# Attention features in a fused performer and mixture kernel: the shift's arithmetic rewritten, one scaling, three copies and one group of sums put elsewhere

## The chip, the core and the metric

The kernel runs on one core of a Trainium2 chip. A core has five engines that run their own instruction queues side by side and wait for each other by semaphores: TensorE (PE, matmuls; its weight loads are shown as PEld), VectorE (DVE), ScalarE (ACT), GpSimd (POOL) and SyncE (SP, which here only issues DMAs). The metric is the device time of one execution in microseconds (us). Before the change it is 640.66 us, the median of three runs (640.45 to 641.06).

## What is computed

Three layers follow each other. The first is linear attention with random features over 2 batches, 8 heads, 576 tokens of 64 numbers, with 128 features:

```python
def phi(x):
    proj = np.einsum('bhsd,md->bhsm', x, omega)
    sq = np.sum(x * x, axis=-1, keepdims=True) / 2.0
    h = proj - sq
    h = h - np.max(h, axis=-1, keepdims=True)
    return np.exp(h) / np.sqrt(m)
q_p, k_p = phi(q_s), phi(k_s)          # q_s, k_s: q and k scaled
kv = einsum('bhsm,bhsd->bhmd', k_p, v); z = sum(k_p, axis=2)
num = einsum('bhsm,bhmd->bhsd', q_p, kv)
den = einsum('bhsm,bhm->bhs', q_p, z)[..., None] + 1e-06
out = num / den
```

The second is a mixture of four experts on the 1152 tokens of width 512 (each: 512 to 1024, relu, 1024 to 512, weighted and summed). The third takes 512 to 2048, multiplies each value by its cosine, and goes back to 512.

## The kernel before, in words

The order of the instructions on each engine is the order in which the Python code is run; generators are advanced by hand, and each `yield` marks a place where other work is put in between. There is no scheduler behind it.

The attention works on eight pairs of heads (`pairs`, line 1139), four tokens per partition, and a ninth part for the tokens that are left over (qL, kL). The loop over `s` from line 1356 is a pipeline: in step `s` it finishes the sums of keys and values of pair `s-1` (`kv_of`, line 1155), turns the queries of pair `s` and the keys of pair `s+1` (`turn_ahead`, line 1279, output `xT`), makes the features of both (`features`, line 1058), and writes the result of pair `s-2`. From `s = 6` on (`first`, line 1259) quanta of the expert layer's matmuls (`dense_quanta`) are put between the attention's.

The features of one pair need a shift per token. GpSimd squares the 64 numbers of each token and adds them in halves down to 16 (`norms_ahead`, lines 1017 and 1021), then multiplies these 16 by a constant (line 1024). VectorE adds the 16 (line 1074), takes the maxima of the projections from PSUM (line 1080), and then forms the shift from a tile `three` of three numbers for each token with two reductions over two neighbouring numbers each (lines 1089 and 1092); the second writes `nb`. ScalarE's exponentials (line 1099, output `phk` or `phq`) take `nb` as their bias. There are 17 such shifts: nine for queries (q0 to q7 and qL) and eight for keys (k0 to k7). The kL part makes its shift otherwise. For the keys of steps before `first`, `shift_later` puts a yield between the maxima and the two reductions, so that on VectorE the next step's copy of `xT` comes in between.

In the expert layers each quantum is six matmuls. `token_sums` (line 338) makes sums of blocks of the tokens (tiles T1, T2 and so on, each as a high and a low part), and one of its two calls, for the columns that begin at 1, is advanced a quantum at a time once attention is over (lines 1444 and 1445). `Second.ahead` stages the inputs of the second matmuls (`sth` on ScalarE at line 749, `stl` on VectorE at line 752).

Of the kernel before, what the change touches and what calls it, by code (L numbers as in the profile page):

```python
# [12 lines left out]
ACTF = mybir.ActivationFunctionType  # L13
ALU = mybir.AluOpType
AX = mybir.AxisListType
# [11 lines left out]
def performer_moe_kernel(ctx, tc, q, k, v, omega, probs, w1, w2, w_in, w_out, out):  # L27
    nc = tc.nc
# [16 lines left out]
    SC = float(D) ** -0.25  # L45
# [16 lines left out]
    def bank(name):  # L62
        return ps.tile([P, 512], F32, tag="ps", name=name)
# [218 lines left out]
    def tokens(n, ks, cols):  # L282
        return [t[:, ks, HALF * n + cols.start : HALF * n + cols.stop, :] for t in x_t]
# [4 lines left out]
    def whole(r, parts):  # L288
        h, l = (x.bitcast(F32) for x in parts)
        nc.vector.tensor_tensor(out=r, in0=h, in1=l, op=ALU.add)  # L290

    def minus(dst, x, y):
        nc.vector.tensor_tensor(out=dst, in0=x, in1=y, op=ALU.subtract)  # L293
# [5 lines left out]
    def less(r, n, ks, cols):  # L299
        h, l = (x.bitcast(F32) for x in tokens(n, ks, cols))  # L300
        minus(r, h, r)
        nc.vector.tensor_tensor(out=r, in0=r, in1=l, op=ALU.add)
# [35 lines left out]
    def token_sums(cols):  # L338

        r1, r2 = spare(cols)  # L340
        whole(r2, tokens(0, LO, cols))
        whole(r1, tokens(1, LO, cols))
        if not cols.start:
            yield
        minus(r1, r1, r2)
        yield
        parts = sum_out(1, r1, cols)
        next(parts)
        yield
        yield from parts  # L350
        less(r1, 1, HI, cols)
        yield
        yield from rest_sums(r1, r2, cols)
# [596 lines left out]
    with tc.tile_pool(name="at1", bufs=1) as at1, tc.tile_pool(name="at2", bufs=2) as at2:  # L950
# [63 lines left out]
        def norms_ahead(nm, t):  # L1014

            x2 = at2.tile([P, 2 * R, D], F32, tag=f"x2{nm[0]}", name=f"x2_{nm}")
            nc.gpsimd.tensor_tensor(out=x2, in0=t, in1=t, op=ALU.mult)
            w = D
            while w > 16:
                w //= 2  # L1020
                nc.gpsimd.tensor_tensor(
                    out=x2[:, :, 0:w], in0=x2[:, :, 0:w], in1=x2[:, :, w : 2 * w], op=ALU.add
                )
            nc.gpsimd.tensor_scalar(
                out=x2[:, :, 0:w], in0=x2[:, :, 0:w], scalar1=-SC * SC / 2, scalar2=None, op0=ALU.mult
            )
            sqs[nm] = x2[:, :, 0:w]

        def turn(nm, t, pieces=1):
# [28 lines left out]
        def features(nm, turned, phi, squares=None, shift_later=False):  # L1058

            nb = at2.tile([P, 2 * R], F32, tag=f"nb{nm}"[:3], name=f"nb_{nm}")  # L1060
            pjs = [bank(f"pj_{nm}_{g}") for g in range(2)]
            for i in range(R):
                c = slice(i * P, (i + 1) * P)
                for z, (x_, y) in enumerate([(turned, ws)] + [(squares, minus_norm)] * (squares is not None)):
                    for g, pj in enumerate(pjs):
                        r = slice(g * D, (g + 1) * D)
                        nc.tensor.matmul(
                            pj[:, i * M : (i + 1) * M], x_[r, c], y[r, :],
                            start=z == 0, stop=z == (squares is not None),
                        )  # L1070
            yield
            three = at2.tile([P, 2 * R, 3], F32, tag=f"th{nm[0]}", name=f"three_{nm}")
            def square_sum():
                nc.vector.tensor_reduce(out=three[:, :, 1], in_=sqs.pop(nm), op=ALU.add, axis=AX.X)

            if squares is None and nm != "q0":
                square_sum()
            for g, pj in enumerate(pjs):
                to = (nb if squares is not None else three[:, :, 0])[:, g : 2 * R : 2]
                nc.vector.tensor_reduce(  # L1080
                    out=to, in_=pj.rearrange("p (a m) -> p a m", m=M), op=ALU.max, axis=AX.X,
                    negate=squares is not None,
                )
            if shift_later:
                yield
            if squares is None:
                if nm == "q0":
                    square_sum()
                nc.vector.tensor_reduce(
                    out=three[:, :, 2], in_=three[:, :, 0:2], op=ALU.add, axis=AX.X, negate=True  # L1090
                )
                nc.vector.tensor_reduce(out=nb, in_=three[:, :, 1:3], op=ALU.add, axis=AX.X)
            yield
            order = [g + 2 * i for g in range(2) for i in range(R)]
            if squares is not None:
                order.insert(1, order.pop(R))
            for ix in order:
                i, g = divmod(ix, 2)
                nc.scalar.activation(  # L1099
                    phi[:, ix, :], pjs[g][:, i * M : (i + 1) * M], ACTF.Exp, bias=nb[:, ix : ix + 1]  # L1100
                )
# [38 lines left out]
        NPR = len(pairs)  # L1140
        xss, phks, phqs, kts, qts = {}, {}, {}, {}, {}

        kv = [at1.tile([P, 2, B, D + 1], F32, name=f"kv{hp}") for hp in range(NP)]
# [11 lines left out]
        def kv_of(i):  # L1155
            b, hp = pairs[i]
            ve, phk = ves[i % 2], phks.pop(i)
            kvp = room.pop() if room else bank(f"kv_{i}")
            kvp = kvp[:, 4 * (D + 1) : 6 * (D + 1)].rearrange("p (h e) -> p h e", h=2)
            for h in range(2):  # L1160
                for r in range(R):
                    column_halves(kvp[:, h, :], phk[:, h * R + r, :], ve[:, h * R + r, :], h == r == 0, False)
            yield
            for h in range(2):
                n = 2 * hp + h
                column_halves(kvp[:, h, :], phiL[:, n, :], veL[:, n, b, :], False, h == 1)
            yield
            nc.vector.tensor_copy(out=kv[hp][:, :, b, :], in_=kvp)

        pTs = {}  # L1170
        room = []
# [77 lines left out]
        for b in range(B):  # L1249
            nc.sync.dma_start(  # L1250
                out=pr[:, b * R : (b + 1) * R, :],
                in_=probs[b * S : b * S + SB, :].rearrange("(p r) e -> p r e", r=R),
            )
            nc.sync.dma_start(
                out=pr[b * L : (b + 1) * L, NTILE - 1, :], in_=probs[b * S + SB : (b + 1) * S, :]
# [3 lines left out]
        first = 6  # L1259
# [47 lines left out]
        def k_features(s, shift_later=False):  # L1307
            phks[s] = at2.tile([P, 2 * R, M], F32, tag="phk", name=f"phk_{s}")
            return features(f"k{s}", turned.pop(("k", s)), phks[s], shift_later=shift_later)
# [45 lines left out]
        ks, ns = iter(()), iter(())  # L1355
        for s in range(NPR + 3):
# [4 lines left out]
            else:  # L1361
# [28 lines left out]
                if 2 <= s <= NPR + 1:  # L1390
                    b, hp = pairs[s - 2]
                    px = put_x(f"{s - 2}", hp, xss.pop(s - 2), b * R, R)
                qs = q_features(s) if s <= NPR else iter(())
                ks = k_features(s + 1, s < first) if s + 1 < NPR else iter(())
                next(qs, None)
                next(ks, None)
                next(px, None)
# [34 lines left out]
            if s == first:  # L1432
                nc.vector.reciprocal(out=psum_, in_=psum_)
                nc.vector.tensor_tensor(
                    out=pn, in0=pr, in1=psum_.to_broadcast([P, NTILE, E]), op=ALU.mult
# [40 lines left out]
```

## Time and profile before

| what | value |
|---|---|
| median of three runs | 640.66 us |
| the profiled execution | 640.92 us |
| its span, first to last instruction | 639.1 us |
| TensorE's granted clock, mean | 0.999 of full speed |
| busy share of the span: PE, DVE, ACT, POOL | 99%, 76%, 55%, 27% |
| first matmul of the expert layers (g at line 549) | starts at 52.3 us |

Shares over the whole span say little here, since the change touches only the first 100 us. A table of the engines' busy time by stretches of 10 us is therefore read first, then the chain of waits within the first 100 us, then the order of time around single instructions. A busy PE counts modelled ends of matmuls, so idle time in PE is also seen in the spacing of their starts.

### The profile page before, as it was taken

The page shows a single profiled execution, that of the slowest core. Times are in us where ns is not written, and L with a number is a line of the kernel's source. Part 1 is how long each engine was busy: PE and PEld are TensorE (multiplying, and loading weights), DVE is VectorE, ACT ScalarE, POOL GpSimd, SP SyncE. Part 2 cuts the span into 40 slices and gives each one's busy share as a digit, 9 for nine tenths or more (in the row PEclk, how much of TensorE's full clock was granted, in tenths as well). Part 3 has the DMA queues.
Part 4 walks back from the last instruction along what each step waited for, and adds up shares of the span by engine and source line. Part 5 has one row for each costly group of instructions (what it writes and reads, how often), then busy time and mean ns, then how long its engine had stood idle before and what let it go on. Part 6 is the DMA issues. An engine that isn't in the chain of part 4 may idle for free.

```text
span 639.1 us, 10296 instructions
## 1 busy us (share of the span) xinstructions
PE 632.7 (99%) x3871; PEld 536.3 (84%) x3871; DVE 488.7 (76%) x877; ACT 353.3 (55%) x686; POOL 174.4 (27%) x217
## 2 busy tenths in 40 slices
PE   9999999999999999999999999999999999999997
PEld 8889988988888888888888888888888888888887
DVE  6998588789688688598687697699698772687842
ACT  6898664365346454354443455544457973476821
POOL 7899752033332333323333232310000000000000
PEclk9999999999999999999999999999999999999999
DMA  7644431313446433446334435301250002500111
GB/s 184 169 123 144 134 99 32 101 67 132 132 148 206 141 113 135 133 141 220 133 99 132 143 125 211 131 34 67 94 202 34 2 0 96 234 2 2 49 50 49
DMA packets 55442, 70.97 MB, mean 111 GB/s; under 512 B 15201, under 2 KB 40033, under 8 KB 55393
## 3 DMA queue, kind: packets, MB, share of 16 engines
q1 hardware_dynamic: 46800, 40.92, 20.3%
q0 software_dynamic: 8448, 29.37, 13.2%
q8 instruction: 30, 0.49, 0.3%
q14 instruction: 20, 0.16, 0.1%
q10 hardware_dynamic: 144, 0.03, 0.0%
HBM read 55.36 MB, written 14.94 MB: 110 GB/s over the span
## 4 chain that ended last, share of the span: by engine, by line
PE 86%; ACT 4%; DVE 4%; POOL 3%; issue 1%; DMA 1%; DVEq 0%; ACTq 0%; POOLq 0%
PE g L779 44%; PE g_odd L585 4%; PE g_1c L549 2%; PE g_0a L549 2%; PE g_3a L549 2%; PE g_2a L549 2%; PE g_1a L549 2%; PE g_2c L549 2%; PE g_3c L549 2%; PE g_0c L549 2%; ACT phk L1099 1%; PE g_0d L549 1%; PE g_0b L549 1%; PE g_3e L549 1%; PE g_3b L549 1%
## 5 line engine op out<-in xcount | busy, mean ns | idle before, releaser
L749 ACT ACTIVATE sth<-h 128x512 fp32r<-128x512 f32 (+1 forms) x111 | 60.3, 554 | 80.1 <-PE g L779 67.2
L258 POOL TENSOR_TENSOR c<-c 128x512 uint32<-128x512 uint32 x32 | 47.2, 1475 | 86.8 <-issue 34.0
L752 DVE SCALAR_TENSOR_TENSOR stl<-h,sth 128x512 fp32r<-128x512 f32 (+1 forms) x72 | 49.1, 697 | 26.7 <-ACT sth L749 26.6
L779 PE MATMUL g<-v2h,stl 128*128 128x512 f32 (+1 forms) x110 | 42.5, 386 | 0.6 <-DVE stl L752 0.6
L779 PE MATMUL g<-v3h,sth 128*128 128x512 f32 (+1 forms) x110 | 42.9, 390 | 0.0
L779 PE MATMUL g<-v0h,sth 128*128 128x512 f32 (+1 forms) x110 | 42.7, 388 | 0.0
L779 PE MATMUL g<-v1h,sth 128*128 128x512 f32 (+1 forms) x110 | 42.7, 388 | 0.0
L779 PE MATMUL g<-v2h,sth 128*128 128x512 f32 (+1 forms) x110 | 42.5, 386 | 0.0
L779 PE MATMUL g<-v0h,stl 128*128 128x512 f32 (+1 forms) x110 | 42.5, 386 | 0.0
L779 PE MATMUL g<-v3h,stl 128*128 128x512 f32 (+1 forms) x110 | 42.4, 386 | 0.0
L779 PE MATMUL g<-v1h,stl 128*128 128x512 f32 (+1 forms) x110 | 42.4, 386 | 0.0
L779 PE MATMUL g<-v1l,sth 128*128 128x512 f32 (+1 forms) x110 | 42.4, 385 | 0.0
L779 PE MATMUL g<-v0l,sth 128*128 128x512 f32 (+1 forms) x110 | 42.4, 385 | 0.0
L779 PE MATMUL g<-v3l,sth 128*128 128x512 f32 (+1 forms) x110 | 42.4, 385 | 0.0
L779 PE MATMUL g<-v2l,sth 128*128 128x512 f32 (+1 forms) x110 | 42.4, 385 | 0.0
L293 DVE TENSOR_TENSOR stl<-h,sth 128x512 fp32r<-128x512 f32 (+1 forms) x39 | 22.8, 593 | 19.3 <-ACT sth L749 19.1
L451 DVE SCALAR_TENSOR_TENSOR c<-c 128x512 f32<-128x512 f32 (+1 forms) x38 | 25.0, 662 | 11.9 <-ACT c L449 11.8
L448 ACT ACTIVATE c<-h 128x512 f32<-128x512 f32 x32 | 19.9, 622 | 19.9 <-DVE h L626 19.9
L805 DVE SCALAR_TENSOR_TENSOR acc<-g,pn,acc 128x512 f32<-128x512 f32 x27 | 20.1, 744 | 6.5 <-PE g L779 6.5
L779 PEld LDWEIGHTS g<-v2h,stl 128*128 128x128 f32 x110 | 20.7, 188 | 5.1 <-DVE stl L752 1.0
L779 PEld LDWEIGHTS g<-v0h,stl 128*128 128x128 f32 x110 | 20.7, 188 | 4.4 <-DVE stl L752 0.3
L779 PEld LDWEIGHTS g<-v3h,stl 128*128 128x128 f32 x110 | 20.7, 188 | 4.2
(437 smaller groups left out, 1877.3 us busy)
## 6 DMA issues: line engine op xcount, KB each, us to landing
rv<-in_moe_w_dram SPq DMA_DIRECT2D x16, 512.0 KB, 4.0
c<-in_moe_w_in_dram POOLq DMA_DIRECT2D x16, 512.0 KB, 4.1
c<-in_moe_w_out_dram POOLq DMA_DIRECT2D x16, 512.0 KB, 3.9
kt<-in_k_dram SPq DMA_DIRECT2D x8, 256.0 KB, 3.7
qt<-in_q_dram SPq DMA_DIRECT2D x8, 256.0 KB, 4.0
ve<-in_v_dram SPq DMA_DIRECT2D x16, 128.0 KB, 4.2
ra_2as<-in_moe_w_dram SPq DMA_DIRECT2D x8, 256.0 KB, 3.3
out_dram<-acc SPq DMA_DIRECT2D x7, 256.0 KB, 2.3
```

Source lines behind the costliest of these rows:

```text
L258: nc.gpsimd.tensor_tensor(out=total, in0=t, in1=lw, op=ALU.add)
L293: nc.vector.tensor_tensor(out=dst, in0=x, in1=y, op=ALU.subtract)
L448: nc.scalar.activation(vv, src, ACTF.Copy, bias=0.25, scale=INV_2PI)
L451: nc.vector.scalar_tensor_tensor(out=vv, in0=kk, scalar=ROUND, in1=vv, op0=ALU.subtract, op1=ALU.subtract)
L549: nc.tensor.matmul(dst, x[:, o], y[:, kk], start=start and n == 0, stop=stop and n == 3 * kn - 1, skip_group_check=reopen,)
L585: nc.tensor.matmul(g, x[:, kk], w[:, :, :, kk, :], start=n == 0, stop=n == 3 * KD - 1)
L749: nc.scalar.activation(hi, src, ACTF.Relu if self.e < E else ACTF.Copy)
L752: nc.vector.scalar_tensor_tensor(out=to, in0=src, scalar=0.0, in1=hi.bitcast(F32), op0=ALU.max, op1=ALU.subtract)
L779: nc.tensor.matmul(g, x, y[:, o : o + w], start=n == 0, stop=n == 3 * FT - 1)
L805: nc.vector.scalar_tensor_tensor(out=acc[t], in0=src, scalar=p_, in1=acc[t], op0=ALU.mult, op1=ALU.add)
L1099: nc.scalar.activation(phi[:, ix, :], pjs[g][:, i * M : (i + 1) * M], ACTF.Exp, bias=nb[:, ix : ix + 1])
```

## The change

Four things are changed.

1. GpSimd's multiplication by the constant (line 1024) is gone, 17 instructions. The constant is put into VectorE's two instructions of the shift, which become two `scalar_tensor_tensor` in place of two `tensor_reduce`. Both take two inputs from the tile `three`, which lies in SBUF.
2. The copy of the sums of keys and values out of PSUM (line 1168) is made by ScalarE for pairs 1, 2 and 3 (in steps 2, 3 and 4), by VectorE for the others as before.
3. `shift_later` isn't passed any more: the keys' shift stands right behind their maxima in all steps.
4. In `token_sums`, for the columns that begin at 1, there is one more yield ahead of `less(r1, 1, HI, cols)`.

```diff
@@ token_sums
         next(parts)
         yield
         yield from parts
+        if cols.start:
+            yield
         less(r1, 1, HI, cols)
@@ norms_ahead
-            nc.gpsimd.tensor_scalar(
-                out=x2[:, :, 0:w], in0=x2[:, :, 0:w], scalar1=-SC * SC / 2, scalar2=None, op0=ALU.mult
-            )
             sqs[nm] = x2[:, :, 0:w]
@@ features
-                nc.vector.tensor_reduce(
-                    out=three[:, :, 2], in_=three[:, :, 0:2], op=ALU.add, axis=AX.X, negate=True
-                )
-                nc.vector.tensor_reduce(out=nb, in_=three[:, :, 1:3], op=ALU.add, axis=AX.X)
+                for out, x, op in ((three[:, :, 2], three[:, :, 0], ALU.add), (nb, three[:, :, 2], ALU.subtract)):
+                    nc.vector.scalar_tensor_tensor(
+                        out=out, in0=three[:, :, 1], scalar=-SC * SC / 2, in1=x, op0=ALU.mult, op1=op
+                    )
@@ kv_of
-            nc.vector.tensor_copy(out=kv[hp][:, :, b, :], in_=kvp)
+            if i in (1, 2, 3):
+                nc.scalar.activation(kv[hp][:, :, b, :], kvp, ACTF.Copy)
+            else:
+                nc.vector.tensor_copy(out=kv[hp][:, :, b, :], in_=kvp)
@@ the loop over s
-                ks = k_features(s + 1, s < first) if s + 1 < NPR else iter(())
+                ks = k_features(s + 1) if s + 1 < NPR else iter(())
```

On VectorE, at the turn from step 1 to step 2, the order before is this (the numbers behind the names are buffers; `pj_k` are the projections, `tp` the turned inputs, `rd` and `xs` the division, `tq` the turned features):

```order
L1080 TENSOR_REDUCE three_k_441<-pj_k_1_426 128x4
L1303 COPY xT_522<-tp_0_504 128x8x64
L1089 TENSOR_REDUCE three_k_441<-three_k_441 128x8
L1092 TENSOR_REDUCE nb_k_424<-three_k_441 128x8
L1110 TENSOR_SCALAR rd_0_557<-num_1_464 128x4
L1110 TENSOR_SCALAR rd_1_559<-num_0_473 128x4
L1112 RECIPROCAL rd_0_557<-rd_0_557 128x4
L1112 RECIPROCAL rd_1_559<-rd_1_559 128x4
L1114 TENSOR_TENSOR xs_463<-num_1_464,rd_0_557 128x4x64
L1114 TENSOR_TENSOR xs_463<-num_0_473,rd_1_559 128x4x64
L1168 COPY kv_141<-num_1_464 128x2x65
L1182 COPY pT_0_566<-tq_0_539 128x512
```

The same place of VectorE's queue after the change:

```order
L1079 TENSOR_REDUCE three_k_436<-pj_k_1_421 128x4
L1089 SCALAR_TENSOR_TENSOR three_k_436<-three_k_436 128x8
L1089 SCALAR_TENSOR_TENSOR nb_k_419<-three_k_436 128x8
L1305 COPY xT_517<-tp_0_499 128x8x64
L1109 TENSOR_SCALAR rd_0_550<-num_1_459 128x4
L1109 TENSOR_SCALAR rd_1_552<-num_0_468 128x4
L1111 RECIPROCAL rd_0_550<-rd_0_550 128x4
L1111 RECIPROCAL rd_1_552<-rd_1_552 128x4
L1113 TENSOR_TENSOR xs_458<-num_1_459,rd_0_550 128x4x64
L1113 TENSOR_TENSOR xs_458<-num_0_468,rd_1_552 128x4x64
L1184 COPY pT_0_559<-tq_0_532 128x512
```

The shift stands ahead of the copy of `xT`, its two instructions are of another kind, and the copy of `kv` has left this queue.

On GpSimd, for the queries of pair 3 and the keys of pair 4, before:

```order
L1017 TENSOR_TENSOR x_q_621<-qt_3_484 128x512
L1021 TENSOR_TENSOR x_q_621<-x_q_621 128x8x32
L1021 TENSOR_TENSOR x_q_621<-x_q_621 128x8x16
L1024 TENSOR_SCALAR x_q_621<-x_q_621 128x8x16
L1017 TENSOR_TENSOR x_k_626<-kt_0_482 128x512
L1021 TENSOR_TENSOR x_k_626<-x_k_626 128x8x32
L1021 TENSOR_TENSOR x_k_626<-x_k_626 128x8x16
L1024 TENSOR_SCALAR x_k_626<-x_k_626 128x8x16
```

And after:

```order
L1019 TENSOR_TENSOR x_q_616<-qt_3_479 128x512
L1023 TENSOR_TENSOR x_q_616<-x_q_616 128x8x32
L1023 TENSOR_TENSOR x_q_616<-x_q_616 128x8x16
L1019 TENSOR_TENSOR x_k_620<-kt_0_477 128x512
L1023 TENSOR_TENSOR x_k_620<-x_k_620 128x8x32
L1023 TENSOR_TENSOR x_k_620<-x_k_620 128x8x16
```

Each set of squares is three instructions in place of four.

On VectorE at the end of attention, where `h` names a free buffer that `token_sums` uses for its sums and `c` and `acc` hold inputs of the second matmuls, before:

```order
L293 TENSOR_TENSOR h<-h 128x2x384
L752 SCALAR_TENSOR_TENSOR stl<-c_97,sth 128x512
L134 TENSOR_TENSOR T1l<-h,T1h 128x2x384
L293 TENSOR_TENSOR h<-xh,h 128x2x384
L302 TENSOR_TENSOR h<-h,xl 128x2x384
L752 SCALAR_TENSOR_TENSOR stl<-c_97,sth 128x256
L752 SCALAR_TENSOR_TENSOR stl<-acc_100,sth 128x256
L293 TENSOR_TENSOR h<-h 128x2x384
L134 TENSOR_TENSOR T2l<-h,T2h 128x2x384
```

And after:

```order
L293 TENSOR_TENSOR h<-h 128x2x384
L754 SCALAR_TENSOR_TENSOR stl<-c_97,sth 128x512
L134 TENSOR_TENSOR T1l<-h,T1h 128x2x384
L754 SCALAR_TENSOR_TENSOR stl<-c_97,sth 128x256
L754 SCALAR_TENSOR_TENSOR stl<-acc_100,sth 128x256
L293 TENSOR_TENSOR h<-xh,h 128x2x384
L302 TENSOR_TENSOR h<-h,xl 128x2x384
L293 TENSOR_TENSOR h<-h 128x2x384
L134 TENSOR_TENSOR T2l<-h,T2h 128x2x384
```

The two `stl` now stand ahead of the two sums of `less`. On ScalarE the evacuation `acc` (line 803) likewise moves ahead of `T2h`. The queues of PE and SP are the same in both kernels.

## Rows read from the trace of the kernel before

**Rows 1.** The page's first two lines: the span, and each engine's busy us (share).

```profile
span 639.1 us, 10296 instructions
PE 632.7 (99%) x3871; PEld 536.3 (84%) x3871; DVE 488.7 (76%) x877; ACT 353.3 (55%) x686; POOL 174.4 (27%) x217
```

**Rows 2.** Stretches of 10 us: length, busy us of each engine (instructions), PE clock, DMA.

```profile
20.00:30.00 10.00, 9.73 (x212) 8.57 (x208) 9.31 (x34) 8.87 (x31) 8.95 (x14) 1.00 0.62 166
...
40.00:50.00 10.00, 9.90 (x223) 9.01 (x220) 9.66 (x34) 9.55 (x32) 9.18 (x13) 1.00 0.27 78
...
70.00:80.00 10.00, 10.00 (x106) 9.24 (x107) 5.52 (x20) 5.55 (x16) 7.08 (x7) 1.00 0.52 157
```

**Rows 3.** The chain of waits, first 120 us: start us, us, engine, tile, line.

```profile
21.13 0.68 DVE xT L1303
...
28.11 0.60 DVE xT L1303
...
30.06 0.20 DVE kv L1168
...
36.19 2.24 ACT phk L1099 x8
...
48.70 0.66 DVE xT L1303
```

**Rows 4.** Groups of POOL's instructions, first 72 us: xcount | busy us, mean ns.

```profile
L1017 POOL TENSOR_TENSOR x_q<-qt 128x512 f32<-128x512 f32 x8 | 8.3, 1040 | 0.5
...
L1021 POOL TENSOR_TENSOR x_q<-x_q 128x256 f32<-128x256 f32 x9 | 6.6, 731 | 0.7
...
L1024 POOL TENSOR_SCALAR x_q<-x_q 128x128 f32<-128x128 f32 x9 | 4.8, 529 | 0.8
L1024 POOL TENSOR_SCALAR x_k<-x_k 128x128 f32<-128x128 f32 x8 | 4.2, 530 | 0.7
L1021 POOL TENSOR_TENSOR x_q<-x_q 128x128 f32<-128x128 f32 x9 | 4.1, 459 | 0.7
```

**Rows 5.** The order of time near 32 us: start us, us, engine, line, instruction.

```profile
30.93 0.53 POOL L1024 TENSOR_SCALAR x_k<-x_k 128x128 f32<-128x128 f32 x1
...
31.55 1.04 POOL L1017 TENSOR_TENSOR x_q<-qt 128x512 f32<-128x512 f32 x1
...
32.28 0.17 DVE L1089 TENSOR_REDUCE three_q<-three_q 128x8 f32<-128x16 f32 x1
```

**Rows 6.** The order of time near 56 us.

```profile
54.99 2.53 POOL L134 TENSOR_TENSOR w1l<-ra_2p,w1h 128x512 fp32r<-128x512 f32 x2
...
56.33 0.20 DVE L1433 RECIPROCAL psum__161<-psum__161 128x9 f32<-128x9 f32 x1
...
56.57 1.00 DVE L1434 TENSOR_TENSOR pn<-pr,psum__161 128x36 f32<-128x36 f32 x1
```

**Rows 7.** The order of time near 88 us.

```profile
87.54 3.37 POOL L193 TENSOR_TENSOR ra_1s<-ra_1s 128x256 f32<-128x256 f32 x4 [1.20 <-DMA ra_1s<-in_moe_w_dram]
87.61 2.70 DVE L752 SCALAR_TENSOR_TENSOR stl<-c,sth 128x256 fp32r<-128x256 f32 x3
```

**Rows 8.** ScalarE's small copies, in the order of time.

```profile
4.54 0.38 ACT L1049 ACTIVATE xT_k<-tp_k 128x256 f32<-128x256 f32 x1 [0.41 <-PE tp_k L1037]
...
41.49 0.26 ACT L1431 ACTIVATE psum__161<-psum__161 128x9 f32<-128x9 f32 x1
```

**Rows 9.** The order of time from 98 to 103 us; in brackets idle time and its releaser.

```profile
98.00 0.39 PE L779 MATMUL g<-v2l,sth 128*128 128x512 f32 x1
98.49 0.42 DVE L752 SCALAR_TENSOR_TENSOR stl<-c,sth 128x256 fp32r<-128x256 f32 x1
...
98.96 0.50 PE L779 MATMUL g<-v2h,stl 128*128 128x512 f32 x1 [0.57 <-DVE stl L752]
...
100.03 0.95 DVE L134 TENSOR_TENSOR T2l<-h,T2h 128x768 fp32r<-128x768 f32 x1
...
102.60 0.33 PE L549 MATMUL g_0d<-T2l,w1h 128*128 128x384 f32 x1
```

## The prediction, made before the changed kernel was run

> **What bounds the kernel now.** I read the page's first lines, then stretches of 10 us, then the chain of waits over the first 120 us, and last the order of time around the touched instructions. The page shows TensorE busy for 632.7 of 639.1 us [rows 1], but the part that the change touches ends at about 100 us. From 52.3 us on (the table), quanta of expert matmuls fill TensorE: in 70 to 80 us it is busy for 10.00 of 10 us, VectorE for 5.52 [rows 2]. There, a late shift costs nothing until it is later than the quanta put around it. Ahead of that, in steps 1 to 5 of the attention, all engines are nearly full: in 40 to 50 us VectorE 9.66, ScalarE 9.55, GpSimd 9.18 of 10 us; in 20 to 30 us 9.31, 8.87 and 8.95 [rows 2]. The chain runs mostly over VectorE there, with a stretch on ScalarE (the exponentials at 36.19) [rows 3]. A step is 6.98 us between the copies of xT at 21.13 and 28.11, and (48.70 - 28.11) / 3 = 6.86 us over the next three [rows 3]. So what VectorE gains or loses in a step of this phase moves the step almost one to one, and TensorE passes all of it on to the end.
>
> **Part 1, the shift's two instructions.** Removed from GpSimd: 17 multiplications of 0.53 us [rows 4] with a gap of 31.55 - 31.46 = 0.09 us each [rows 5], 10.5 us of a queue that is full. For TensorE this is worth nothing that I can see: squares are ready before VectorE asks for them, and where GpSimd's work shows up late, from 50 us on, TensorE is full without it [rows 2]. The bound on the other side is a step that did hang on GpSimd: two multiplications in it, 2 x 0.62 = 1.2 us.
>
> On VectorE two reductions of 0.17 us [rows 5] become two instructions of another kind. By elements they cost as much. What differs is that both inputs lie in SBUF, and the trace shows what that does beside GpSimd. At 56.33 a reciprocal with one SBUF input took 0.20 us beside GpSimd's subtraction. Right behind it, a multiplication of 36 elements with two SBUF inputs took 1.00 us, from 56.57 to 57.57, while the subtraction ended at 54.99 + 2.53 = 57.52 [rows 6]. At 87.61, three stl of 256 elements, two SBUF inputs each, took 0.90 us apiece beside four sums of GpSimd [rows 7], where the same instruction alone took 0.42 [rows 9]; the two engines took turns. A reduction isn't held: at 32.28 it took 0.17 us in the middle of GpSimd's squaring (31.55 to 32.59) [rows 5]. So VectorE's new instruction waits until GpSimd's instruction in flight ends, and 8 elements wait as long as 256.
>
> [...]
>
> The price of one pair: GpSimd's squares are now 1.04, 0.73 and 0.46 us [rows 4] with three gaps of 0.08, 2.47 us in all. If one of them is in flight, the mean rest of it is (1.04² + 0.73² + 0.46²) / (2 x 2.47) = 0.37 us. The second instruction needs the first one's result and so comes about when GpSimd starts its next instruction. If it loses, it waits for most of that one, 0.61 us on the mean (0.71 by the weights of the three, less 0.1 in which it wasn't ready). The turns at 87.61 say that it can lose; for an instruction as short as this no row tells, so I take half: 0.37 + 0.30 = 0.67 us. The ends for a pair are 0 (GpSimd idle) and 1.04 + 0.73 = 1.77 us.
>
> How often GpSimd is in flight: the squares of one step now need 2 x 2.47 = 4.94 us of about 7.7, so 0.64 of the time once it has caught up; until it has, I take 0.9 (before, it is full). Pairs on the path are k0 to k6 and q0 to q5, 13; q6, k7, q7 and qL lie under the quanta and cost nothing as long as phq and phk still start in time (the longest single wait there is one piece of a weight subtraction, 2.53 / 2 = 1.27 us [rows 6]; the four on the path after all would be at most 5 us). Seven pairs at 0.9 and six at 0.64: 0.67 x (6.3 + 3.8) = 6.8 us. Some of it fills time in which VectorE waits anyway: it idles for 0.69 and 0.34 us in the two stretches [rows 2], so about 2 us over 10 to 50 us; I take half, -1.0.
>
> **Part 2, three copies to ScalarE.** VectorE loses 0.20 us of the chain in steps 2 to 4 [rows 3]. ScalarE gains a copy of 130 elements, between its 9 elements in 0.26 and 256 in 0.38 us [rows 8], I take 0.3. In steps 2 and 3 ScalarE has 1.13 us idle in ten [rows 2], so the gain stands, -0.4; in step 4 the chain is on ScalarE [rows 3], so between +0.3 and -0.2, I take 0.
>
> **Part 3, the keys' shift ahead of xT.** The same instructions in another order: VectorE's sum doesn't change. xT comes later by two instructions, 2 x 0.17 [rows 5], plus the waits above, and TensorE's projections of the queries with it; VectorE has the division and pT to do before it asks for them. phk may start earlier by as much. Taken as 0, with -0.4 and +0.4 in each of four steps as bounds.
>
> **Part 4, token sums.** At 98.00 TensorE starts a matmul and the next at 98.96; the spacing where nothing waits is 0.23 us, so the wait for stl costs 0.73 us [rows 9]. With the two stl ahead of the two sums of less (about 0.95 us each, like T2l [rows 9]) they are done 1.9 us earlier, and the wait goes: -0.73. Next late is T2l: VectorE does the same work up to its end at 100.98, and TensorE, now 0.73 earlier, reads it at 102.60 - 0.73 = 101.87 [rows 9]. 0.9 us of room; were it gone, each us late would cost one. So the range of this part is -0.73 to 0.
>
> **Sum.** 640.92 (the profiled execution, 639.1 of span and 1.8 around it) + 6.8 - 1.0 - 0.4 - 0.73 = 645.6. That execution is 0.26 above the median, so **645.3 us**.
>
> **Rivals.**
> - Second instruction always loses to GpSimd: 0.98 per pair, 0.98 x 10.1 = 9.9, less 2.1 for the other terms: 648.5. For it: the strict turns at 87.61. Against: there the queued work was 256 elements long.
> - Second never loses: 0.37 x 10.1 = 3.7, less 2.1: 642.3. For it: GpSimd's gap of 0.09 us between dependent instructions [rows 5] lets VectorE in. Against: the next squaring needs nothing from the one before it.
> - Hidden: ScalarE sets the pace of steps 4 and 5 [rows 3], GpSimd runs ahead after three steps and is idle when the shifts come. Then half of the pairs pay 0.37, about +2.0 less 2.1: 640.6, no change. Against: VectorE is as full as ScalarE in these steps.
> - The other side, faster: 8 elements pass in GpSimd's gaps or aren't held at all, and GpSimd's queue did set the pace of a step. Then -0.73 - 0.6 for three copies, and up to -1.2 for the multiplications: 638.1; without the last it would be 639.3. It decides in favour of the change if a pair costs less than about 0.13 us (1.33 / 10.1) on the path. Against: the 36 elements that took 1.00 us [rows 6].
>
> **How the numbers follow.** A measurement of this kernel can tell 0.2%, 1.3 us, so faster is below 639.4 and slower above 641.9. Forecast (643.4 to 647.4) 0.42; always loses 0.17; never loses 0.17; hidden 0.13, of which 0.08 stay within 0.2% and the rest is split; faster 0.11, a third of it within 0.2%. This gives faster 0.10, same 0.12, slower 0.78. The range that leaves out at most 2 in 10 goes from 640.6 to 649.0; the likeliest case's own is 643.4 to 647.4.
>
> **What would show it.** Line 1089's mean in the changed profile well above 0.17 us, about 0.3 to 0.9, its longest over 1 us, with ends just behind ends of GpSimd's squares; steps between copies of xT of 7.3 to 8.3 us in place of 6.9; the first expert matmul (52.3 us before, in the table) some 5 us later; GpSimd idle between sets of squares; TensorE's spacing of 0.23 us unbroken where stl comes in before the first blocks. The forecast is wrong if line 1089 stays at 0.17 beside GpSimd, or if its waits are there and the steps stay at 6.9 us, or if a new wait for T2l takes back part 4.

## The result, and the profile after

| kernel | median | runs |
|---|---|---|
| before, on the same chip | 640.87 us | 6 (640.45 to 641.06) |
| changed | 644.38 us | 6 (642.66 to 646.39) |

The changed kernel is slower by 0.56%: the ratio is 1.0056, with a 95% interval of 1.0039 to 1.0073. The prediction was 645.3 us, range 640.6 to 649.0. The runs of the changed kernel also spread six times as wide as those of before; a second profile, below, shows what differs between two of its executions.

The profiled execution took 646.39 us, the longest of the six. Its page begins so (compare [rows 1]):

```profile
span 644.6 us, 10278 instructions
PE 633.3 (98%) x3871; PEld 536.8 (83%) x3871; DVE 496.9 (77%) x874; ACT 353.7 (55%) x689; POOL 165.4 (26%) x200
```

GpSimd's busy time is 9.0 us shorter; VectorE, with three instructions fewer, has 8.2 us more, and the span is 5.5 us longer. One of the stretches of 10 us, as in [rows 2]:

```profile
20.00:30.00 10.00, 8.61 (x202) 7.75 (x201) 9.72 (x24) 6.66 (x24) 7.29 (x11) 1.00 0.48 134
```

Between 20 and 30 us VectorE is busier (9.72 against 9.31 us) with 24 instructions instead of 34, while TensorE falls from 9.73 to 8.61 and ScalarE from 8.87 to 6.66. Fewer instructions in more busy time means that some of them take longer, and the rows of line 1089 show which: its instructions wait inside their own duration. The groups of line 1089, first 56 us (count | busy us, mean ns of one):

```profile
L1089 DVE SCALAR_TENSOR_TENSOR three_q<-three_q 128x8 f32<-128x8 f32 x6 | 3.5, 575 | 0.2
L1089 DVE SCALAR_TENSOR_TENSOR nb_k<-three_k 128x8 f32<-128x8 f32 x7 | 3.3, 477 | 0.4
L1089 DVE SCALAR_TENSOR_TENSOR three_k<-three_k 128x8 f32<-128x8 f32 x7 | 3.2, 459 | 0.2
L1089 DVE SCALAR_TENSOR_TENSOR nb_q<-three_q 128x8 f32<-128x8 f32 x6 | 1.6, 260 | 0.2
```

These 26 instructions of 13 pairs take 11.6 us. At 0.17 us each, which they take without GpSimd's squares (experiment 10), they would take 4.4, so 7.2 us are waits. The chain of waits (start us, us, engine, tile, line), where [rows 3] had copies of `xT` 6.9 us apart:

```profile
24.91 0.60 DVE xT L1305
...
28.60 0.74 DVE three_q L1089
...
32.76 0.60 DVE xT L1305
...
40.40 0.60 DVE xT L1305
```

The steps are now 7.85 and 7.64 us, and the shift itself stands in the chain, 0.74 us at a time. The first expert matmul starts at 58.1 us, 5.7 us later than before.

### The profile page after: what moved, and what is told of

Same layout as the page of the kernel before. It is cut to its first block, busy times and chain, and to the rows that moved or that the text cites. A ratio compares the mean times of both kernels' runs of the same rounds, so it can differ in the third digit from the quotient of the medians.

```text
span 644.6 us, 10278 instructions
## 1 busy us (share of the span) xinstructions
PE 633.3 (98%) x3871; PEld 536.8 (83%) x3871; DVE 496.9 (77%) x874; ACT 353.7 (55%) x689; POOL 165.4 (26%) x200
## 4 chain that ended last, share of the span: by engine, by line
PE 92%; DVE 7%; issue 0%; ACT 0%; DVEq 0%
PE g L781 46%; PE g_odd L587 4%; PE g L551 3%; PE g_0c L551 3%; PE g_1c L551 2%; PE g_3a L551 2%; PE g_2c L551 2%; PE g_2a L551 2%; PE g_1a L551 2%; PE g_3c L551 2%; PE g_0a L551 2%; DVE three_k L1079 1%; PE g_0d L551 1%; PE g_0e L551 1%; PE g_0b L551 1%; PE g_3e L551 1%
## 5 line engine op out<-in xcount | busy, mean ns | idle before, releaser
L781 PEld LDWEIGHTS g<-v1h,stl 128*128 128x128 f32 x110 | 20.7, 188 | 4.2
```

Of the source, the lines that this page charges most:

```text
L781: nc.tensor.matmul(g, x, y[:, o : o + w], start=n == 0, stop=n == 3 * FT - 1)
```

## The experiments

Each time is the median on a chip, beside runs of the kernel before on the same chip (640.92 to 640.95 us). In the traces I also counted TensorE's 3871 matmuls and compared the start of the same matmul in two kernels. By 10 us this differs from one profiled execution to the next by up to 1.3 us, so differences are taken from there on.

**1. Everything but the shift.** The changed kernel with part 1 undone, so parts 2 to 4 alone.

```diff
+            nc.gpsimd.tensor_scalar(
+                out=x2[:, :, 0:w], in0=x2[:, :, 0:w], scalar1=-SC * SC / 2, scalar2=None, op0=ALU.mult
+            )
-                for out, x, op in ((three[:, :, 2], three[:, :, 0], ALU.add), (nb, three[:, :, 2], ALU.subtract)):
-                    nc.vector.scalar_tensor_tensor(
-                        out=out, in0=three[:, :, 1], scalar=-SC * SC / 2, in1=x, op0=ALU.mult, op1=op
-                    )
+                nc.vector.tensor_reduce(
+                    out=three[:, :, 2], in_=three[:, :, 0:2], op=ALU.add, axis=AX.X, negate=True
+                )
+                nc.vector.tensor_reduce(out=nb, in_=three[:, :, 1:3], op=ALU.add, axis=AX.X)
```

> The changed kernel with part 1 undone: GpSimd multiplies again and VectorE forms the shift with two reductions; parts 2 to 4 stay. Lock theory (the loss of 3.5 us lies in the two-input instructions that wait for GpSimd): 640.2 us, 639.7 to 640.9, no instruction of the shift over 0.2 us. Rival (the loss lies in the order: copies on ScalarE, keys' shift ahead of xT, token sums later): 643 to 645.

Measured: 641.0 us, ratio 1.0 (0.9992 to 1.0009), 0.1 us above the range that was expected and far from the rival's. The whole loss belongs to part 1; parts 2 to 4 together change nothing that the interval can tell.

**2. The kind alone.** The kernel before with two `tensor_tensor` of the same inputs in place of the two reductions; GpSimd keeps its multiplications.

```diff
-                nc.vector.tensor_reduce(
-                    out=three[:, :, 2], in_=three[:, :, 0:2], op=ALU.add, axis=AX.X, negate=True
-                )
-                nc.vector.tensor_reduce(out=nb, in_=three[:, :, 1:3], op=ALU.add, axis=AX.X)
+                for out, x, op in ((three[:, :, 2], three[:, :, 0], ALU.add), (nb, three[:, :, 2], ALU.subtract)):
+                    nc.vector.tensor_tensor(out=out, in0=three[:, :, 1], in1=x, op=op)
```

> The kernel before with one thing changed: the two reductions of the shift become two tensor_tensor with two SBUF inputs, and GpSimd still multiplies. Lock theory: GpSimd is never idle there, so nearly all of 13 pairs on the path wait, 0.4 to 0.9 us each: 646 to 651 us, more than the changed kernel. Rival (the loss needs one of the other edits): 640.9.

Measured: 642.9 us (641.23 to 646.6), ratio 1.0044 (1.0023 to 1.0064). The direction is right, the size is a miss: the median lies below the expected 646 to 651 us, and below the changed kernel. In its trace five of the 13 pairs wait for next to nothing (0.02 us at most), and one waits far longer than the others. Its two instructions, in the order of time:

```profile
44.10 2.51 POOL L134 TENSOR_TENSOR w02l<-ra_0p,w02h 128x512 fp32r<-128x512 f32 x2
...
44.21 1.21 DVE L1090 TENSOR_TENSOR three_k<-three_k 128x8 f32<-128x8 f32 x1
...
45.45 1.18 DVE L1090 TENSOR_TENSOR nb_k<-three_k 128x8 f32<-128x8 f32 x1
```

Both instructions of the pair waited, each for one half of the weight subtraction, 2.1 us in all. TensorE ran dry behind it, with 0.24 us busy in a stretch of 2 us, and its granted clock fell to 0.50 (stretches of 2 us; after TensorE's busy time come PEld, DVE, ACT, POOL, then the clock):

```profile
46.00:48.00 2.00, 0.24 (x1) 0.24 (x2) 2.00 (x9) 1.33 (x6) 1.92 (x3) 0.85 0.05 16
48.00:50.00 2.00, 2.00 (x16) 1.80 (x16) 1.97 (x5) 1.33 (x5) 1.75 (x4) 0.50 1.02 307
50.00:52.00 2.00, 2.00 (x23) 1.64 (x23) 1.01 (x3) 0.82 (x4) 1.84 (x3) 0.50 0.79 200
```

This execution took 646.6 us, and its 13 pairs waited 5.1 us. Counted by matmuls, TensorE is 1.9 us behind the kernel before ahead of this pair and 6.6 us behind it at 54.7 us, though VectorE's shift waited only 2.7 us in between. The idle time and the clock at its lower level thus cost more than the waits. Of the ten runs four took 645.8 to 646.6 us; three of these had a mean granted clock of 0.995 to 0.997, the fourth 1.000. The shortest run took 641.23 us; that it had no such wait was not traced.

**3. The relief alone.** The kernel before without GpSimd's multiplications (the squares stay unscaled, so this part of the computation is left out).

```diff
-            nc.gpsimd.tensor_scalar(
-                out=x2[:, :, 0:w], in0=x2[:, :, 0:w], scalar1=-SC * SC / 2, scalar2=None, op0=ALU.mult
-            )
```

> The kernel before without GpSimd's 17 multiplications; the squares stay unscaled, so the shift has another value. Theory that GpSimd's queue sets no pace in the kernel before: 640.9 us, within 0.5. Rival (it sets the pace of a step or two): 639.7 or less.

Measured: 639.98 us, ratio 0.9986 (0.9977 to 0.9995): a miss, GpSimd's relief is worth 0.95 us. Counted by matmuls, 0.75 us of it come at one place, the wait near 98 us [rows 9]. VectorE's part in it begins 14 us earlier. Before:

```profile
84.12 1.07 DVE L752 SCALAR_TENSOR_TENSOR stl<-c,sth 128x256 fp32r<-128x256 f32 x1 [0.88 <-ACT sth L749]
...
85.11 1.51 DVE L752 SCALAR_TENSOR_TENSOR stl<-acc,sth 128x256 fp32r<-128x256 f32 x1
```

In this run:

```profile
82.86 0.51 DVE L752 SCALAR_TENSOR_TENSOR stl<-c,sth 128x256 fp32r<-128x256 f32 x1 [0.88 <-ACT sth L749]
...
83.28 1.51 DVE L752 SCALAR_TENSOR_TENSOR stl<-acc,sth 128x256 fp32r<-128x256 f32 x1
...
85.79 1.12 DVE L752 SCALAR_TENSOR_TENSOR stl<-c,sth 128x256 fp32r<-128x256 f32 x3
...
86.88 3.26 POOL L193 TENSOR_TENSOR ra_1s<-ra_1s 128x256 f32<-128x256 f32 x4 [0.92 <-DMA ra_1s<-in_moe_w_dram]
...
89.20 0.88 DVE L1134 TENSOR_TENSOR xl<-tx_L,xh 128x128 fp32r<-128x128 f32 x4 [1.30 <-ACT xh L1131]
...
96.96 0.39 PE L779 MATMUL g<-v2l,sth 128*128 128x512 f32 x1
...
97.19 0.48 PE L779 MATMUL g<-v2h,stl 128*128 128x512 f32 x1
```

The first `stl` takes 0.51 us instead of 1.07. Here it starts ahead of GpSimd's subtraction for `w1l` (83.04 us); before, it started inside the first half of it (83.61 to 84.91 us). From 83.28 us on VectorE is 1.8 us earlier than before, TensorE only 1.0 us; 0.56 of these 0.8 us are this instruction's. The three `stl` of [rows 7] also come ahead of GpSimd's four sums and take 1.12 us, not 2.70, but that gain is lost at once: VectorE then idles for 1.30 us until ScalarE has `xh`, and behind it is 1.8 us earlier, as it was ahead of them. TensorE's wait near 98 us is gone, the spacing at this place is 0.23 us. Why the two engines stand differently to each other at 83 us was not followed further back.

**4. Reductions without scaling.** The changed kernel with the two reductions, and without the scaling of the squares anywhere.

```diff
-                for out, x, op in ((three[:, :, 2], three[:, :, 0], ALU.add), (nb, three[:, :, 2], ALU.subtract)):
-                    nc.vector.scalar_tensor_tensor(
-                        out=out, in0=three[:, :, 1], scalar=-SC * SC / 2, in1=x, op0=ALU.mult, op1=op
-                    )
+                nc.vector.tensor_reduce(
+                    out=three[:, :, 2], in_=three[:, :, 0:2], op=ALU.add, axis=AX.X, negate=True
+                )
+                nc.vector.tensor_reduce(out=nb, in_=three[:, :, 1:3], op=ALU.add, axis=AX.X)
```

> The changed kernel with two reductions in place of the two scalar_tensor_tensor, and no multiplication anywhere; the squares stay unscaled. Everything else is as in the changed kernel, GpSimd's lighter load too. Lock theory: 640.2 us, as without part 1, the difference of about 4 us to the changed kernel being the price of the waits. Rival (lighter GpSimd or order is at fault): 643 to 645.

Measured: 640.06 us, ratio 0.9989 (0.9981 to 0.9998). With GpSimd's squares as in the changed kernel, the kind of the two instructions costs 644.38 - 640.06 = 4.3 us. Against experiment 1, which differs by the multiplications alone, the relief is again 0.94 us. Here the three `stl` take 1.11 us, the first one 0.64.

**5 to 7. Parts 4, 2 and 3 alone**, each as in the change, put into the kernel before.

```diff
+        if cols.start:
+            yield
```

> The kernel before with part 4 alone (token sums a quantum later). Theory, from the trace of the changed kernel: TensorE's wait of 0.73 us for stl at 98 us goes, and 0.48 us of it comes back at g_0c's last matmul, where TensorE then waits for VectorE's additions of h: about -0.25, 640.7 us against 640.95. The prediction's own price: the whole 0.73 stays, 640.2 us. Third: nothing stays, 640.95.

Measured: 640.73 us, ratio 0.9997 (0.9988 to 1.0006).

```diff
+            if i in (1, 2, 3):
+                nc.scalar.activation(kv[hp][:, :, b, :], kvp, ACTF.Copy)
```

> The kernel before with part 2 alone (three copies of kv on ScalarE). By the prediction -0.4 (two steps of 0.20 us off VectorE's path, the third nothing): 640.55 us. Rival, since parts 2 to 4 together measured the same as before: ScalarE's 0.33 us in steps 2 to 4 come ahead of exponentials that are waited for, +0.3 to +0.6: 641.3 to 641.6 us.

Measured: 641.07 us, ratio 1.0002 (0.9993 to 1.001).

```diff
-                ks = k_features(s + 1, s < first) if s + 1 < NPR else iter(())
+                ks = k_features(s + 1) if s + 1 < NPR else iter(())
```

> The kernel before with part 3 alone (keys' shift right behind their maxima). By the prediction 0, 640.95 us. Rival: xT is later by two reductions of 0.17 us in each of four steps with nothing to show for it, up to 4 x 0.2 = +0.8: 641.75 us. Other rival: phk's exponentials start earlier and ScalarE gives its stretch of the chain back, -0.4: 640.55 us.

Measured: 641.05 us, ratio 1.0002 (0.9993 to 1.0011). The three medians lie -0.2, +0.1 and +0.1 us from before, which adds up to experiment 1; each interval is about half a us to either side, so the single signs aren't shown. For parts 2 and 4 the traces tell more (next section).

**8. The sum behind the maxima.** In the changed kernel's trace the shift met GpSimd in the same way in several steps (order of time: start us, us, engine, line; in brackets idle time and its releaser):

```profile
27.10 0.28 DVE L1073 TENSOR_REDUCE three_q<-x_q 128x8 f32<-128x128 f32 x1
...
27.45 1.04 POOL L1019 TENSOR_TENSOR x_q<-qt 128x512 f32<-128x512 f32 x1 [2.03 <-DVE three_q L1073]
...
28.57 1.29 POOL L1023 TENSOR_TENSOR x_q<-x_q 128x256 f32<-128x256 f32 x2
28.60 0.73 DVE L1089 SCALAR_TENSOR_TENSOR three_q<-three_q 128x8 f32<-128x8 f32 x1
29.37 0.17 DVE L1089 SCALAR_TENSOR_TENSOR nb_q<-three_q 128x8 f32<-128x8 f32 x1
```

VectorE's sum (line 1073) reads the squares and so gives their buffer back; GpSimd had idled 2.03 us for it and starts the next squaring at once. The two maxima take VectorE 1.2 us more, GpSimd's squaring with its gap 1.12 us; so the shift comes 0.03 us after GpSimd has begun the piece of 0.73 us, and waits for all of it. The same happens at 31.63, 36.44 and 39.46 us. If the sum sets the meeting in this way (a lock-step: the two engines go on at a fixed offset), it is not left to chance, and moving the sum should move it. Here the sum stands right ahead of the shift.

```diff
-            if squares is None and nm != "q0":
-                square_sum()
...
-                if nm == "q0":
-                    square_sum()
+                square_sum()
```

> The changed kernel with VectorE's sum of the squares behind the maxima for every pair, as for q0 alone so far. Theory (the wait is set by a lock-step: the sum hands the buffer back, GpSimd starts its next squaring at once, and the shift comes a fixed time after the sum): the sum is now right ahead of the shift, so the shift meets the start of a squaring of 1.04 us and waits 0.9 to 1.0 us per pair where it now waits 0.56; 0.4 more over 10 to 13 pairs, or somewhat less where two buffers leave GpSimd further ahead: +2 to +4 us against the changed kernel, 646.5 to 648.5 us. Rival (the shift meets GpSimd's queue at random): as the changed kernel, 644.4 us.

Measured: 647.36 us, ratio to before 1.01 (1.0086 to 1.0114), 2.9 us above the changed kernel (644.51 us on that chip, below). The order of time:

```profile
44.40 0.17 DVE L1086 SCALAR_TENSOR_TENSOR three_q<-three_q 128x8 f32<-128x8 f32 x1
44.45 1.04 POOL L1019 TENSOR_TENSOR x_q<-qt 128x512 f32<-128x512 f32 x1
44.61 0.91 DVE L1086 SCALAR_TENSOR_TENSOR nb_q<-three_q 128x8 f32<-128x8 f32 x1
```

Now it is the second instruction that meets the squaring and takes 0.91 us; the same 0.90 or 0.91 stands in six pairs in a row from 27.57 to 47.81 us. The place of the wait followed the place of the sum, as the lock-step says. The waits of its 13 pairs sum to 8.1 us, 0.9 to 2.5 us more than in the two profiles of the changed kernel. Part of the 2.9 us is TensorE's granted clock, which was 0.79, 0.50 and 0.85 in the three stretches of 2 us from 24 us on, after TensorE had been busy for 1.19 and 0.82 us in the two ahead of them; after 1.09 us from 48 us on it stayed at 1.00, so what lowered it isn't shown. The second of those two and the stretch at 0.50:

```profile
22.00:24.00 2.00, 0.82 (x16) 0.57 (x15) 1.90 (x3) 1.60 (x7) 1.84 (x3) 1.00 0.82 265
...
26.00:28.00 2.00, 2.00 (x18) 1.78 (x16) 1.93 (x5) 0.53 (x2) 1.05 (x2) 0.50 0.47 128
```

The chain of waits runs over TensorE there. The same three groups of matmuls, at the lower clock and a few steps later at a clock of 1.00:

```profile
24.41 1.42 PE pj_q L1066 x16
25.83 1.71 PE pj_k L1066 x16
27.54 1.06 PE tx L1118 x4
...
49.46 1.16 PE pj_q L1066 x16
50.62 1.24 PE pj_k L1066 x16
51.86 0.60 PE tx L1118 x4
```

That is 4.19 us against 3.00, so about 1.2 us of this execution are the clock's, and the waits' own share is less than the +2 to +4 us that were expected. All four runs had a mean clock of 0.995 to 0.997.

**9. The sum earlier.** The changed kernel with the sum one quantum ahead, right behind `pT`'s copy.

```diff
-            yield
             three = at2.tile([P, 2 * R, 3], F32, tag=f"th{nm[0]}", name=f"three_{nm}")
...
                 square_sum()
+            yield
```

> The changed kernel with VectorE's sum of the squares one quantum earlier (behind pT's copy, ahead of the rest of the quantum's instructions), everything else as it is. Theory (lock-step through the buffer that the sum hands back): the shift now comes later in GpSimd's set of squares than the start of its 0.73 us piece, in the 0.46 us piece or behind the set, so 0 to 0.4 us per pair where it now waits 0.56; over 10 to 13 pairs 1 to 3 us less than the changed kernel: 641.5 to 643.5 us. Rival (the shift meets GpSimd at random, so the place of the sum is nothing): as the changed kernel, 644.4 us.

Measured: 643.9 us, ratio to before 1.0048 (1.0036 to 1.0061). The changed kernel on the same chip:

> The changed kernel once more, as the measure for the others of this chip: 644.4 us. No theory differs on it.

Measured: 644.51 us, ratio 1.0056 (1.0043 to 1.0069). So -0.6 us: the direction of the theory, less than its -1 to -3, and with overlapping intervals not settled by the times. Between 10 us and the first expert matmuls its TensorE loses 3.2 us to the kernel before, the changed kernel's 5.3 and, in its second profile, 3.6. The trace says why the gain is small:

```profile
33.27 1.04 POOL L1019 TENSOR_TENSOR x_q<-qt 128x512 f32<-128x512 f32 x1 [1.71 <-DVE three_k L1072]
34.39 1.29 POOL L1023 TENSOR_TENSOR x_q<-x_q 128x256 f32<-128x256 f32 x2
34.51 0.65 DVE L1089 SCALAR_TENSOR_TENSOR three_q<-three_q 128x8 f32<-128x8 f32 x1
...
37.25 0.26 DVE L1089 SCALAR_TENSOR_TENSOR three_k<-three_k 128x8 f32<-128x8 f32 x1
```

Both buffers come back together and GpSimd does two sets in a row. The queries' shift falls into the first set and still pays 0.48 us; the keys' shift falls near the end of the piece of 0.73 us in the second and pays 0.09. The lock-step has another phase, and it isn't gone.

The second profile of the changed kernel (644.69 us) shows what differs between two of its executions. Line 1089, first 56 us:

```profile
L1089 DVE SCALAR_TENSOR_TENSOR nb_k<-three_k 128x8 f32<-128x8 f32 x7 | 3.6, 520 | 0.4
L1089 DVE SCALAR_TENSOR_TENSOR three_q<-three_q 128x8 f32<-128x8 f32 x6 | 2.5, 413 | 0.2
L1089 DVE SCALAR_TENSOR_TENSOR three_k<-three_k 128x8 f32<-128x8 f32 x7 | 2.3, 331 | 0.2
L1089 DVE SCALAR_TENSOR_TENSOR nb_q<-three_q 128x8 f32<-128x8 f32 x6 | 1.6, 260 | 0.2
```

10.0 us against 11.6 in the first, 1.6 us less waiting in an execution 1.7 us shorter. Which of the two instructions waits, and when, differs between the two profiles: the wait of 0.56 us for the whole piece of 0.73 us stands in four pairs in a row in the first, and in three pairs, two of them in a row, in the second. That this makes the spread of the times isn't shown by two profiles; the five runs on this chip lie within 0.6 us.

**10. GpSimd still.** The changed kernel without GpSimd's squares and sums; VectorE sums a constant tile instead (this part of the computation is left out). VectorE's instructions are the same, kind by kind.

```diff
-            nc.gpsimd.tensor_tensor(out=x2, in0=t, in1=t, op=ALU.mult)
...
+            sqs[nm] = still
```

> The changed kernel without GpSimd's squares and their sums: VectorE sums a constant tile of the same shape in their place, so its instructions are the same, kind by kind, and GpSimd is idle in the attention. Theory (the price is the wait for GpSimd): each shift instruction takes 0.17 us, and the 4.3 us of the kind go, and some tenths for GpSimd's relief as well: 639 to 640 us. Rival (the kind costs by itself, in gaps around it or by a longer way through the engine): 643 to 644.4 us.

Measured: 640.52 us, ratio to before 0.9993 (0.9984 to 1.0002), 4.0 us less than the changed kernel beside it: 0.5 us above the theory's range, far from the rival's. The instructions of the keys' shift, min/median/max in ns:

```profile
L1083 DVE SCALAR_TENSOR_TENSOR three_k<-three_k x8: 169/171/172, 9.5 to 57.5; 128x8 f32<-128x8 f32 x8
L1083 DVE SCALAR_TENSOR_TENSOR nb_k<-three_k x8: 169/170/173, 9.7 to 57.7; 128x8 f32<-128x8 f32 x8
```

The queries' shift takes 0.17 us too, up to 52 us. Behind that three of its pairs still meet GpSimd's weight subtractions, and their longest instruction takes 1.21 us. With experiment 4 three corners of a square are measured: reductions beside GpSimd's squares 640.06, the new kind beside them 644.4 to 644.5, the new kind without them 640.52 us; the fourth, reductions without squares, was not run. With either of the two alone the kernel is no slower than before; the price is their meeting. Single instructions show it too. In the kernel before, none of the 34 reductions of the shift took over 0.174 us, and one of them stood in the middle of the squaring [rows 5]; the new kind took 0.73 us at 28.60 us, beside GpSimd's additions. With one of its two inputs in PSUM an instruction wasn't held: the two of `xs` (`num` in PSUM, `rd` in SBUF) took 0.76 us at 36.03 us in the kernel before, inside GpSimd's additions (35.76 to 37.02 us), and 0.75 us at 22.67 us in this run, where GpSimd did nothing from 20 to 30 us.

**11. No squares.** Since a token's squares are the same for all its features, they cancel: exp(p - s - max(p - s)) = exp(p - max(p)). The kernel before with part 4, and with minus the maximum as the exponentials' bias; GpSimd's squares, VectorE's sums and both shift instructions of these pairs are gone.

```diff
-            nc.gpsimd.tensor_tensor(out=x2, in0=t, in1=t, op=ALU.mult)
-                square_sum()
-                nc.vector.tensor_reduce(
-                    out=three[:, :, 2], in_=three[:, :, 0:2], op=ALU.add, axis=AX.X, negate=True
-                )
-                nc.vector.tensor_reduce(out=nb, in_=three[:, :, 1:3], op=ALU.add, axis=AX.X)
-                to = (nb if squares is not None else three[:, :, 0])[:, g : 2 * R : 2]
+                to = nb[:, g : 2 * R : 2]
-                    negate=squares is not None,
+                    negate=True,
```

> The kernel before with part 4 and without the squares of the feature maps on GpSimd and VectorE: the bias of the exponentials is minus the maximum of the projection, since the squares cancel between a token's feature and its own maximum. VectorE loses three instructions per pair (0.20 + 0.17 + 0.17 us with gaps, about 0.6 us), GpSimd the whole set (some 3 us per pair). If VectorE's sum alone sets the step: 13 pairs x 0.6 = -7.8 us: 633 us. If ScalarE takes over (it idles 0.45 to 1.1 us in ten before, so 2 to 4 us over the five steps): 637 to 638.5 us. If nothing of it was on the path: 640.7 us. I take ScalarE: 637.5 us.

Measured: 638.16 us (637.93 to 638.68), ratio to before 0.9958 (0.9945 to 0.9972). It beats both kernels, by 2.8 and 6.4 us. One stretch of 10 us:

```profile
30.00:40.00 10.00, 9.89 (x223) 8.95 (x222) 8.49 (x21) 9.59 (x33) 2.49 (x2) 1.00 0.74 198
```

VectorE is down to 8.5 of 10 us, TensorE is at 9.9 and ScalarE at 9.6. The chain of waits from 20 to 52 us is on TensorE for the most part, with ScalarE's exponentials of two steps in between, 2.17 us each. So of the 7.8 us (13 pairs at 0.6) that VectorE lost, less than 2.8 reached the end: counted by matmuls, 1.7 us are there at the first expert matmuls, and 0.85 us come near 98 us, where part 4 and GpSimd's lighter load act as well.

## Why the prediction was right, and where it wasn't

**The mechanism (part 1, the kind).** Right. The rows that carried it, 36 elements that took 1.00 us up to a subtraction's end [rows 6] and a reduction of 0.17 us that didn't wait [rows 5], hold for 8 elements too: in the changed profile the new instructions took up to 1.21 us, with 0.17 where nothing held them. The same 36 elements took 0.20 us there, at 63.41 us, with no instruction of GpSimd in flight. The price of a pair was 0.67 us where GpSimd is in flight, 6.8 us for 13 pairs; the two profiles show 7.2 and 5.6 us. The second instruction was taken to lose half of the time: in the first profile it waits in 5 of 13 pairs, 0.52 to 0.55 us each, where 0.61 was taken. But the way to the number was wrong: the prediction averaged over a random meeting, and the traces show one that repeats for a good part of it, set by the buffer that the sum gives back (four pairs in a row in the first profile, six in experiment 8). That the average came near is luck; with the sum elsewhere the same formula would have said the same, and the waits of the 13 pairs were 8.1 us in experiment 8 and 5.2 in experiment 9.

**VectorE's slack (-1.0).** Too small. Counted by matmuls against experiment 10, 5.6 us of waits cost 3.8 us and 7.2 cost 5.5, so 1.7 to 1.8 us are absorbed.

**GpSimd's relief (0).** Beside the reductions this step fails: there the relief is worth 0.95 us (experiments 3 and 4). The prediction looked at the wrong place: whether squares are ready in time, and that TensorE is full from 50 us on. But TensorE still has one wait behind VectorE at 98 us, the one that part 4 was costed by, and VectorE came late there for the most part by what its `stl` at 84 us had waited beside GpSimd (experiment 3), not by [rows 7], where the prediction saw the same waits. In the changed kernel this gain doesn't show. Its first `stl` takes 1.35 us and its three stand beside GpSimd's sums (from 93.09 us) as before, in the first profile:

```profile
93.15 2.72 DVE L754 SCALAR_TENSOR_TENSOR stl<-c,sth 128x256 fp32r<-128x256 f32 x3
```

In the second they take 1.35 and 2.68 us. Against experiment 1, which has the multiplications, TensorE's delay stays at 5.8 us from 90 to 114 us.

**Copies on ScalarE (-0.4).** Measured +0.1, alone (experiment 6); the interval goes down to -0.45. The trace is sharper: counted by matmuls, TensorE stays 0.4 us behind the kernel before from 10 us to the end, at most 0.6 us near 38 us, so in this execution the copies gave nothing. They take 0.33, 0.33 and 0.41 us in the changed kernel, where 0.3 was taken.

**The keys' shift (0).** Measured +0.1, alone, inside its bounds.

**Token sums (-0.73).** The stall went, and most of it came back 9 us later (103.81 to 112.96 us). The changed kernel, in the order of time:

```profile
103.58 0.39 PE L781 MATMUL g<-v2l,sth 128*128 128x512 f32 x1
103.81 0.39 PE L781 MATMUL g<-v2h,stl 128*128 128x512 f32 x1
...
105.59 0.96 DVE L134 TENSOR_TENSOR T2l<-h,T2h 128x768 fp32r<-128x768 f32 x1
...
107.31 0.33 PE L551 MATMUL g_0d<-T2l,w1h 128*128 128x384 f32 x1
...
112.34 0.56 DVE L628 TENSOR_TENSOR h<-g_0c,h 128x384 f32<-128x384 f32 x1
...
112.96 0.44 PE L551 MATMUL g_0c<-T4h,w02h 128*128 128x384 f32 x1 [0.26 <-DVE h L628]
```

The spacing at `stl` is 0.23 us, and T2l ends at 106.55, 0.76 us ahead of its reader: both as predicted. But VectorE does the same work up to 113 us, and its addition to `g_0c` is next late: by the spacing of the matmuls TensorE loses 0.5 us around 112.96, and 0.2 before that around 109.45, where it waits for `xl`. Counted by matmuls, of 0.88 us gained near 98 us 0.16 is left behind 113; in experiment 5, of 0.86 us, 0.13. "Next late is T2l" was the step that failed: the wait had to be followed along VectorE's queue until that engine idles.

**The sum.** By the runs: +3.4 for part 1 (the changed kernel against experiment 1) and about 0 for parts 2 to 4, against +3.5 measured. On the way over experiment 4 part 1 falls into +4.3 for the kind and -0.95 for the relief. That these add up is no check, since each run is a step between the two kernels, and the 4.3 hold the loss of a relief that the changed kernel doesn't show. The prediction had +5.8 for part 1 and -1.1 for parts 2 to 4, together +4.7 on its execution. Part 1 was 2.4 too dear; against that, parts 2 to 4 were booked with 1.1 that did not come. The errors cancel in part, so the total is better than its terms.

Of what the prediction asked to see, line 1089's mean (0.26 to 0.58 us by tile, the longest 1.21), steps of 7.9, 7.6, 7.5 and 7.0 us (the last below the 7.3 to 8.3 that were asked), the later expert matmul and TensorE's unbroken spacing are there. GpSimd idles between sets, 2.03 us at 27.45, and waits there for VectorE.

## What to carry to other kernels

Before moving arithmetic from GpSimd into an instruction of VectorE, count its inputs in SBUF: in these runs a short instruction with two of them often cost what was left of GpSimd's instruction in flight, with 8 elements (up to 1.21 us, where 0.17 is the time without a wait) as with 36 (1.00 against 0.20 us). Look for what starts that GpSimd instruction: if it is a buffer that VectorE itself hands back a little earlier, the two can meet at the same place step after step, and an average over random meetings tells nothing about moving either. And where a reordering takes away one wait for a full engine, follow that engine's queue to its next idle time before the gain is booked.

## What the runs showed that was not expected

- Within one execution the meeting repeats to within 0.01 us: in the first profile of the changed kernel the first instruction of the shift waited 0.56 us in four pairs in a row (28.60 to 39.46 us), and with the sum moved the second one waited 0.73 or 0.74 us in six.
- Behind those four waits the second instruction started each time in the gap between two dependent instructions of GpSimd, which is only about 0.1 us long (1.29 us for the two at 28.57, of 0.73 and 0.46 us [rows 4]), and took 0.17 us.
- Waits of VectorE can cost TensorE more than they last: in experiment 2 TensorE fell back by another 4.7 us over waits of 2.7 us, with its granted clock at 0.50 for three stretches of 2 us.
- The first 10 us differ between the profiled executions of these kernels by up to 1.3 us in the start of TensorE's matmuls; 0.5 us of that stands between the kernel before and experiment 5, whose only edit lies far behind. Differences of about a us between two profiles have to be read from a point behind that.
